# A decode step on one core: TensorE loops over head groups, V gets a single slot, and a group's last sum and mask multiply move behind the next group's first multiply

## The chip, the cores and the metric

The kernel runs on one core of a Trainium2 chip. The time is the device time of one execution in microseconds (us), as the median of several runs. A profile of one execution comes with each kernel; its span (first to last instruction) is 1.1 to 1.3 us shorter than the time.

## The reference

One token of a transformer block is decoded: a layer norm, attention of 32 heads over a cache of 4096 keys and values, and a gated feed-forward part.

```python
x = A_x                                   # (1, 1, 640), bfloat16 as everything
q = layernorm(x) @ wq                     # 32 heads of 128
scores = einsum("bhqd,bhkd->bhqk", q, k_cache) * 128 ** -0.5   # 4096 keys a head
o = einsum("bhqk,bhkd->bhqd", softmax(scores), v_cache)
h = x + o @ wo
out = h + (gelu(n @ w_gate) * (n @ w_up)) @ w_down             # n = layernorm(h), width 1728
```

K and V are 33.6 MB each. With the weights the kernel must read 84.23 MB, and there is only one query row, so every byte is used once.

## The kernel before

The heads are worked in 8 groups of four. A K or V load brings 4 MB, 32 KB to each of 128 partitions; K3 is the K load of group 3. Three slots rotate over all loads; a load into a slot waits until the load three places earlier has been used.

```python
order = [("K", 0), ("V", 0), ("K", 1)]
for G in range(1, NG - 1):
    order += [("K", G + 1), ("V", G)]
order.append(("V", NG - 1))
...   # load n waits for consumed[n - 3]
```

A group has four multiplies on VectorE (`prod`, 128x4096 elements). For each, eight TensorE multiplies with the identity add up the head dimension in part (a "fold"), VectorE sums the rest, and ScalarE takes exponentials in four pieces, each written to its place in a block matrix `p_bd`. The product of these exponentials with V is called P.V; a "head sum" on TensorE then adds up its parts for each head.

Cut to what matters here:

```python
def score_mult(s):
    m = V(tensor_tensor(prod[s % 4], K tile, q))                 # waits: K landed, fold s-4
    folds[s] = T(8 x matmul(ps_f[s % 2], id_b, prod[s % 4]))     # identity loaded 8 times
def score_exp(s):
    reds[s] = V(reduce_sum(sc[s % 4], ps_f[s % 2]))
    for j in range(4):
        A(activation(p_bd[32j:32j+32, G % 2, ..., j], sc[...], Exp, accum_out=RS[...]))
def scores(G):
    for i in range(4):
        score_mult(4 * G + i)
        if i >= 1:
            score_exp(4 * G + i - 1)
    score_exp(4 * G + 3)
...   # program order: scores(G+1), then the P.V product of group G (32 matmuls), then the next group;
...   # group 0's P.V comes before scores(1)
```

After group 3 and after group 7 one half of the heads is normalised and spread for the projection with `wo`. Then follow the second layer norm and the gated part, whose weights are the last loads of the same stream.

The softmax here doesn't subtract the row's maximum and nothing guards it: scores larger than these inputs give would overflow.

## Time and profile before

| | before |
|---|---|
| time, median (lowest to highest) | 203.1 us (202.97 to 203.22) |
| span of the profiled run | 201.9 us |
| HBM bytes read | 84.23 MB, 417 GB/s over the span |
| a group's transfer (K and V) | 19.4 us |
| VectorE busy of that, steady group | 11.5 us |

These lines are from the page of the kernel before: busy time of each engine; the busy tenths and the rate of the DMA engines in 40 equal slices; and the instruction fetches.

```profile
PE 120.4 (60%) x1010; PEld 58.8 (29%) x1010; DVE 101.2 (50%) x106; ACT 61.1 (30%) x273; POOL 5.0 (2%) x14
...
DMA  9999999999999999999999999999999999999992
GB/s 357 414 404 467 428 415 416 422 448 458 430 415 422 415 445 448 435 424 416 422 435 441 438 435 424 416 428 441 448 419 435 399 425 437 419 408 435 412 409 113
...
q8 instruction: 8, 0.13, 0.3%
```

The DMA row is full (9 means 90% or more) from the first slice to the last but one. The windows view gives the busy time of each engine in a stretch. One steady group:

```profile
core 0: us, PE busy (x) PEld busy (x) DVE busy (x) ACT busy (x) POOL busy (x), PEclk, DMA share, GB/s
74.00:93.50 19.50, 11.82 (x72) 5.19 (x72) 11.47 (x8) 7.54 (x34) 0.00 (x0) 0.91 1.01 431
```

The DMA share is 1.01 at 431 GB/s, while no compute engine is busy for more than 12 of 19.5 us. The Trainium skill, "DMA: Bandwidth & Descriptors", section "Where 436 GB/s comes from", puts the ceiling of the ports into SBUF at 435.2 GB/s; this trace runs at 99% of that. The chain of waits that ended last says the same by engine:

```profile
DMA 64%; PE 16%; DVE 14%; issue 3%; SPq 2%
```

The costliest groups of instructions follow (line, engine, operation, shapes, count; busy us and mean ns of one; idle time of the engine just before them and what ended it). VectorE's multiplies waited 31.1 us for K.

```profile
L273 DVE TENSOR_TENSOR prod<-slot,qb 128x4096 bf16<-128x4096 bf16 x32 | 72.4, 2285 | 31.1 <-DMA slot<-in_A_k_cache_dram 31.1
L292 ACT ACTIVATE p_bd<-sc,zero_t 32x32 bf16<-32x32 f32 x128 | 46.4, 362 | 86.3 <-DVE sc L288 85.1
L281 PEld LDWEIGHTS bank<-prod,id_b 128*128 128x128 bf16 x256 | 26.9, 113 | 99.4 <-DVE prod L273 63.1
L288 DVE TENSOR_REDUCE sc<-bank 128x32 f32<-128x512 f32 x32 | 22.0, 688 | 21.4 <-PE bank L281 21.4
```

Last, the timeline of the load queue (SP), the loads V1, K3 and V2, and of VectorE, the first multiply of group 3. The first column is the start in us.

```profile
43.22 0.33 SPq L51 DMA_DIRECT2D slot<-in_A_v_cache_dram  x1
56.43 0.33 SPq L51 DMA_DIRECT2D slot<-in_A_k_cache_dram  x1
69.12 0.33 SPq L51 DMA_DIRECT2D slot<-in_A_v_cache_dram  x1
```

```profile
74.25 4.49 DVE L273 TENSOR_TENSOR prod<-slot,qb 128x4096 bf16<-128x4096 bf16 x2 [2.47 <-DMA slot<-in_A_k_cache_dram]
```

V1 is issued at 43.2 us, long before K2 has landed (about 54 us). V2 is issued 5.1 us before the first multiply on K3 starts.

### The profile page before, as it was taken

Reading aid. Unit: us, or ns where it says so; the run is one execution under the profiler, and the core shown is the slowest. Engines: PE = TensorE matmul, PEld = TensorE weight load, DVE = VectorE, ACT = ScalarE, POOL = GpSimd, SP = SyncE. Lnnn points to the kernel's source line nnn. Section 1 sums busy time; section 2 is a strip of 40 time slices with the busy share of each in tenths; the row PEclk is TensorE's granted clock in tenths of the full one; section 3 lists DMA queues with packets and bytes.
Section 4 is the critical chain, followed back from the end, with each engine's and each line's share of the span. In section 5 each row is a group of like instructions: output and inputs, shape, how many; then the busy total and the mean of one; then the engine's idle time right before and its main releaser. Section 6 shows DMA issues by size and latency. Waiting matters only on the chain.

```text
span 201.9 us, 2505 instructions
## 1 busy us (share of the span) xinstructions
PE 120.4 (60%) x1010; PEld 58.8 (29%) x1010; DVE 101.2 (50%) x106; ACT 61.1 (30%) x273; POOL 5.0 (2%) x14
## 2 busy tenths in 40 slices
PE   0107058537937668690968197727844887467395
PEld 0103023112312233150324032312331344267383
DVE  3201088517979847924791578277708760100221
ACT  2101004620563550670156125603640363100101
POOL 7200000000000000000000000000000000000000
PEclk9999657995799996997599859988995799955555
DMA  9999999999999999999999999999999999999992
GB/s 357 414 404 467 428 415 416 422 448 458 430 415 422 415 445 448 435 424 416 422 435 441 438 435 424 416 428 441 448 419 435 399 425 437 419 408 435 412 409 113
DMA packets 4335, 84.39 MB, mean 418 GB/s; under 512 B 482, under 2 KB 868, under 8 KB 1508
## 3 DMA queue, kind: packets, MB, share of 16 engines
q1 hardware_dynamic: 4322, 84.23, 97.8%
q8 instruction: 8, 0.13, 0.3%
q14 instruction: 3, 0.02, 0.0%
q10 hardware_dynamic: 2, 0.00, 0.0%
HBM read 84.23 MB, written 0.00 MB: 417 GB/s over the span
## 4 chain that ended last, share of the span: by engine, by line
DMA 64%; PE 16%; DVE 14%; issue 3%; SPq 2%
DMA slot<-in_A_k_cache_dram 42%; DVE prod L273 12%; DMA slot<-in_B_w_down_dram 11%; DMA slot<-in_A_v_cache_dram 11%; PE bank L281 11%; PE bank L310 3%; SPq L51 2%; DVE sc L288 2%; PE bank L319 1%; PE bank L447 0%; DVE out_row L460 0%; PE bank L330 0%; DVE RT L329 0%
## 5 line engine op out<-in xcount | busy, mean ns | idle before, releaser
L281 PE MATMUL bank<-prod,id_b 128*128 128x512 bf16 x256 | 75.4, 454 | 50.8 <-DVE prod L273 50.8
L273 DVE TENSOR_TENSOR prod<-slot,qb 128x4096 bf16<-128x4096 bf16 x32 | 72.4, 2285 | 31.1 <-DMA slot<-in_A_k_cache_dram 31.1
L292 ACT ACTIVATE p_bd<-sc,zero_t 32x32 bf16<-32x32 f32 x128 | 46.4, 362 | 86.3 <-DVE sc L288 85.1
L281 PEld LDWEIGHTS bank<-prod,id_b 128*128 128x128 bf16 x256 | 26.9, 113 | 99.4 <-DVE prod L273 63.1
L288 DVE TENSOR_REDUCE sc<-bank 128x32 f32<-128x512 f32 x32 | 22.0, 688 | 21.4 <-PE bank L281 21.4
L292 ACT ACTIVATION_READ_ACCUMULATOR p_bd<-sc,zero_t 32x1 f32 x128 | 23.5, 184 | 0.0
L310 PE MATMUL bank<-slot,p_bd 128*16 128x512 bf16 x256 | 17.3, 379 | 3.1 <-ACT p_bd L292 2.5
L310 PEld LDWEIGHTS bank<-slot,p_bd 128*16 128x16 bf16 x256 | 9.4, 89 | 7.3 <-ACT p_bd L292 3.0
L319 PE MATMUL bank<-po_sb,hs 128*16 128x128 f32 x64 | 8.4, 274 | 1.1 <-ACT po_sb L314 1.1
L348 PE MATMUL bank<-aP,arena 128*128 128x1 bf16 x160 | 6.7, 178 | 3.8 <-DMA arena<-in_A_wo_dram 3.8
L417 PE MATMUL bank<-hlnT,slot 128*128 128x1 bf16 (+1 forms) x140 | 6.7, 176 | 3.2 <-DMA slot<-in_B_w_gate_dram 3.2
L259 PE MATMUL bank<-arena,xlnB 128*32 128x512 bf16 x40 | 3.9, 565 | 7.2 <-DMA arena<-in_A_wq_dram 7.2
L348 PEld LDWEIGHTS bank<-aP,arena 128*128 128x128 bf16 x160 | 6.6, 131 | 3.9 <-DMA arena<-in_A_wo_dram 2.5
L314 ACT COPY po_sb<-bank 128x512 f32<-128x512 f32 x8 | 4.7, 585 | 9.6 <-PE bank L310 9.6
L417 PEld LDWEIGHTS bank<-hlnT,slot 128*128 128x128 bf16 (+1 forms) x140 | 6.3, 118 | 4.1 <-DVE hX L407 3.3
L319 PEld LDWEIGHTS bank<-po_sb,hs 128*16 128x16 f32 x64 | 5.5, 96 | 4.5 <-issue 2.1
L244 ACT ACTIVATE ln<-ln,eps_t 128x1 f32<-128x1 f32 x2 | 0.6, 294 | 20.3 <-DVE ln L242 20.3
L263 DVE CAST qb<-bank 128x512 bf16<-128x512 f32 x1 | 0.7, 692 | 9.6 <-PE bank L259 9.6
L404 DVE TENSOR_TENSOR hT<-xx,bank 128x5 f32<-128x5 f32 x1 | 0.2, 163 | 10.2 <-PE bank L348 10.2
L233 PE MATMUL bank<-one_bf,x_row 1*128 1x1 bf16 x5 | 0.4, 177 | 6.9 <-DMA x_row<-in_A_x_dram 6.9
L259 PEld LDWEIGHTS bank<-arena,xlnB 128*32 128x32 bf16 x40 | 1.6, 136 | 9.1 <-issue 9.0
L334 DVE TENSOR_SCALAR aT<-bank,rz 16x128 bf16<-16x128 f32 x2 | 0.7, 339 | 6.0 <-PE bank L319 6.0
(65 smaller groups left out, 26.3 us busy)
## 6 DMA issues: line engine op xcount, KB each, us to landing
slot<-in_A_k_cache_dram SPq DMA_DIRECT2D x8, 4096.0 KB, 21.4
slot<-in_A_v_cache_dram SPq DMA_DIRECT2D x7, 4096.0 KB, 17.5
arena<-in_A_wq_dram SPq DMA_DIRECT2D x1, 5120.0 KB, 15.4
slot<-in_A_v_cache_dram SPq DMA_DIRECT2D x2, 2048.0 KB, 20.0
arena<-in_A_wo_dram SPq DMA_DIRECT2D x1, 2560.0 KB, 27.3
slot<-in_B_w_gate_dram SPq DMA_DIRECT2D x1, 2160.0 KB, 16.3
arena<-in_A_wo_dram SPq DMA_DIRECT2D x1, 1920.0 KB, 31.5
slot<-in_B_w_up_dram SPq DMA_DIRECT2D x1, 1296.0 KB, 18.4
```

Source lines behind the costliest of these rows:

```text
L51: ev = self.op(eng, lambda e: e.dma_start(out, in_), *deps, dma=True)
L259: i = e.matmul(ps_q[hf][32 * j:32 * j + 32, :], xlnB[:, c, :], wq_j[:, c, j, 4 * hf:4 * hf + 4, :], start=(c == 0), stop=(c == 4))
L263: qa = V(lambda e: e.tensor_copy(qb[:, 0:4, :].rearrange("p g d -> p (g d)"), ps_q[0][:, :]), qd)
L273: m = V(lambda e: e.tensor_tensor(out=prod[:, s % 4, :, :], in0=kt[:, 32 * u:32 * u + 32, :], in1=qb[:, G, :].unsqueeze(1).to_broadcast([1 ...
L281: i = e.matmul(ps_f[s % 2][:, :], id_b[:, :], prod[:, s % 4, :, 16 * b:16 * b + 16], start=(b == 0), stop=(b == 7))
L288: reds[s] = V(lambda e: e.reduce_sum(sc[:, s % 4, :], ps_f[s % 2][:, :].rearrange("p (g d) -> p g d", d=16), axis=AX.X), folds[s], exps.ge ...
L292: x = A(lambda e, j=j: e.activation(p_bd[32 * j:32 * j + 32, G % 2, 32 * (s % 4):32 * (s % 4) + 32, j], sc[32 * j:32 * j + 32, s % 4, :], ...
L310: i = e.matmul(po[a:a + 16, :], p_bd[:, G % 2, 4 * b:4 * b + 4, :].rearrange("p g j -> p (g j)"), vt[:, 4 * b:4 * b + 4, :], start=(b < 4) ...
L314: evs[G] = A(lambda e: e.copy(po_sb[:, G % 2, :], po[:, :]), pvs[G], hds.get(G - 2))
L319: i = e.matmul(ps_a[0:16, 128 * (G // 4):128 * (G // 4) + 128], hs[:, r, 12 - 4 * g:28 - 4 * g], po_sb[:, G % 2, 128 * r:128 * r + 128], s ...
L348: r = e.matmul(ps_p[:, c:c + 1], wo_sb[:, t, i, c::5], aP[:, t, i:i + 1], start=(t == 0 and c == 0 and i == 0), stop=(t == 1 and i == 15), ...
L417: i = e.matmul(ps[0:128 if m < 13 else 64, m:m + 1], ws, hlnT[:, c:c + 1], start=(c == 0 and m == 0), stop=(c == 4), skip_group_check=True)
```

## The change

The change makes the program smaller and takes work out of each group. TensorE's part of groups 1 to 7 becomes a hardware loop that waits on values computed in registers. For that every group must look alike: K has two slots of its own, V has one, the loads go K0 K1 V0 K2 V1 and so on, and group G-1's P.V runs inside group G behind the third fold. The identity stays loaded for a fold. ScalarE takes one 128x128 exponential a group, and VectorE then places it in the block matrix with one mask multiply. The last sum, the exponential and the mask multiply come behind the next group's first multiply. The two half normalisations become one at the end. Cut to its core, in part in words:

```diff
-order = [("K", 0), ("V", 0), ("K", 1)]
+order = [("K", 0), ("K", 1), ("V", 0)]
+k_slot = two slots; v_slot = one slot      # V7 goes to k_slot[0]
+after = mults[4g-5] for K, pvs[g-1] for V  # what a load waits for
...
-for b in range(8): e.matmul(ps_f[s % 2], id_b, prod[...])
+first matmul loads id_b, seven more keep it (held)
...
-for j in range(4): A(activation(p_bd[32j:32j+32, ...], sc[...], Exp, accum_out=RS[...]))   # per quarter group
+exps[G]   = A(activation(pt[:, G % 2, :], sc[:, G % 2, :], Exp, accum_out=RS[:, G]))       # per group
+blocks[G] = V(tensor_tensor(p_bd, pt (broadcast x4), own (mask), mult))                    # 128x512
...
 def scores(G):
     for i in range(4):
         mults[4G+i] = V(tensor_tensor(prod[i], K, q))
         if i >= 1: reduce(G, i - 1)
+        elif G >= 1: probs(G - 1)      # last sum, exponential, mask multiply of the group before
...
+lp = P.loop("tensor", range(1, NG), [head sum of k-2, fold 0, fold 1, fold 2, P.V of k-1, fold 3])
```

## The prediction

> **What bounds the kernel now.** The input stream. The row of DMA busy tenths shows 9 in every slice but the last, and the windows view gives a DMA share of 1.00 and 428 to 435 GB/s in each stretch of about 19.5 us from 55 us to 171.4 us. The bytes are fixed: 84.23 MB read. The Trainium skill, "DMA: Bandwidth & Descriptors", section "Where 436 GB/s comes from", puts the fabric ceiling at 435.2 GB/s; this trace agrees (429 in mid-stream). An estimate from these: 84.23 MB / 432 GB/s = 195 us, plus about 1 us before the first packet, about 1 us lost in the slow first slices (357 GB/s), about 2.7 us from the last landing (199.2) to the end, plus 1.1 us between span (201.9) and time (203.0). Almost nothing is left to win. One head group needs 19.5 us of K and V transfer; VectorE works 11.5 to 12 us of that, TensorE about 12, ScalarE 7. VectorE's idle time is waiting for K (31.1 us).
>
> **What the change removes, adds, moves.**
> - ScalarE: 128 exponentials of 362 ns with 128 accumulator reads become 8: about 5.8 us a group becomes about 0.6. Off the critical path.
> - TensorE: the identity of a fold is loaded once, not 8 times (113 ns each, overlapped). The loop cuts its instructions about in half. Off the path.
> - VectorE: a mask multiply of 128x512 a group, estimated at 0.3 to 0.7 us from the 128x512 cast (0.69 us); 12 becomes about 12.6 us of 19.5.
> - The last sum, the exponential and the mask multiply now stand behind the next group's first multiply, so they and the P·V product wait for the next K.
> - Instruction fetches: 8 packets (0.13 MB) become about 4, worth 0.2 us (estimate: 4 x 0.6 us of one of 16 engines, if the slowest engine gains). Back-branches could refetch (the skill, "Runtime: NRT & Kernel Launch", section "Instruction fetch mechanics", warns of branches that leave the fetched window); no run shows this yet.
>
> **Does the stream run dry?** Two K slots and one V slot: a V load waits for the previous group's P·V, which runs after the third fold of the group whose K has just landed. With multiply 2.28, sum 0.69, fold 1.9 and P·V 1.9 us, the V load is issued 13 to 14 us after K lands; the queue empties 19.5 us after it. That leaves 4 to 5 us of reserve, similar to before, where V loads go out 12 to 15 us after K lands. Tightest is the beginning: groups 0 and 1 run back to back, P·V of group 0 ends near 51, V1 must be queued by about 53. A cold TensorE or a costly loop entry could open a gap of 0 to 2 us there.
>
> **The end.** V7, wo, gate, up and down keep order and bytes. The last down landing (199.2) and the TensorE chain before it (ends 199.1) stay co-critical. One combined finish after V7 replaces the half done early, but wo lands at 177.5, near aP (175.2), with 2 us spare.
>
> **Predicted:** 202.7 us, range 201.9 to 204.0. Faster by over 2%: 0.01; within 2%: 0.95; slower: 0.04.
>
> **What would show it.** DMA 9 in all slices, 429 GB/s in mid-stream; VectorE's wait for K still about 25 to 31 us; no DMA gap near 54 us; ScalarE busy near 20 us instead of 61; fewer instruction packets.
>
> **What would make it wrong.** Loop or register waits costing over 4 us a group, or refetched instructions, so that V loads are issued late and the stream has holes; a stall on entering the loop.

## The result

The changed kernel takes 203.11 us (median of 4 runs, 202.93 to 203.78) against 203.1 us. The ratio is 1.0006, with a 95% interval of 0.9989 to 1.0023: the same.

The page after:

```profile
PE 121.9 (60%) x1002; PEld 36.9 (18%) x778; DVE 105.7 (52%) x114; ACT 12.6 (6%) x33; POOL 2.4 (1%) x8
...
DMA  9999999999999999999999999999999999999992
GB/s 357 415 398 468 429 422 416 422 442 465 377 455 422 422 422 444 429 455 422 422 422 435 442 429 442 429 422 416 448 429 448 393 432 427 427 408 440 409 411 105
...
q8 instruction: 4, 0.07, 0.1%
```

ScalarE's busy time fell from 61.1 to 12.6 us and the weight loads' (PEld) from 58.8 to 36.9, mostly since a fold loads the identity once and not eight times (32 loads of L346 for 256 of L281, below and above); the instruction packets went from 8 to 4. The DMA row and the span did not move. The windows view, first the stretch that turns out to matter and then the steady group:

```profile
50.00:60.00 10.00, 6.00 (x36) 1.24 (x10) 4.68 (x5) 1.08 (x3) 0.00 (x0) 0.88 1.01 421
74.00:93.50 19.50, 12.22 (x72) 2.15 (x44) 11.99 (x9) 1.08 (x3) 0.00 (x0) 0.78 1.00 432
```

The DMA share is 1.00 again in the steady group, and the rate the same. PEclk, the clock granted to TensorE, is lower there (0.78 against 0.91), as it is over the whole span in all four runs (0.79 to 0.81; the kernel before had 0.82 to 0.87 in the runs of e1's rounds). No run here tests whether the change causes that. The chain of waits, and the groups that answer to those shown of before:

```profile
DMA 60%; DVE 20%; PE 11%; SPq 6%; ACT 1%; issue 1%
```

```profile
L377 DVE TENSOR_TENSOR prod<-k_slot,qb 128x4096 bf16<-128x4096 bf16 x32 | 73.0, 2285 | 43.4 <-DMA k_slot<-in_A_k_cache_dram 43.4
...
L369 DVE TENSOR_REDUCE sc<-bank 128x32 f32<-128x512 f32 x32 | 21.9, 686 | 3.8 <-PE bank L167 3.8
L346 PEld LDWEIGHTS bank<-prod,id_b 128*128 128x128 bf16 x32 | 3.1, 98 | 102.5 <-DVE prod L377 99.5
...
L394 DVE TENSOR_TENSOR p_bd<-pt,own 128x512 bf16<-128x512 bf16 x8 | 5.5, 693 | 4.5 <-ACT pt L392 4.5
...
L392 ACT ACTIVATE pt<-sc,zero_t 128x128 bf16<-128x128 f32 x8 | 3.2, 402 | 71.7 <-DVE sc L369 71.7
```

The mask multiply (L394) takes 693 ns. VectorE's wait for K grew from 31.1 to 43.4 us, and its sums' wait for folds shrank from 21.4 to 3.8: the late last sum turned one wait into the other. Together 52.5 us of idle before, 47.2 after; VectorE's busy time grew by 4.5 us and a wait of 4.5 us for the exponential is new. Nothing of this shows in the time. Now the load queue, V1, K3 and V2, and the first multiplies on K2 and K3:

```profile
50.53 0.33 SPq L59 DMA_DIRECT2D v_slot<-in_A_v_cache_dram  x1
50.91 0.89 SPq L59 DMA_DIRECT2D k_slot<-in_A_k_cache_dram  x1
67.75 0.33 SPq L59 DMA_DIRECT2D v_slot<-in_A_v_cache_dram  x1
```

```profile
54.76 2.29 DVE L377 TENSOR_TENSOR prod<-k_slot,qb 128x4096 bf16<-128x4096 bf16 x1 [4.75 <-DMA k_slot<-in_A_k_cache_dram]
...
74.20 2.29 DVE L377 TENSOR_TENSOR prod<-k_slot,qb 128x4096 bf16<-128x4096 bf16 x1 [6.89 <-DMA k_slot<-in_A_k_cache_dram]
```

K3 is used at 74.20 us, as before (74.25). But V1 is issued at 50.5 us and not at 43.2. The packet records of the trace (not shown; they are in the trace file) hold sixteen 4-byte packets at the end of each load. Taken as one for each of the 16 DMA engines, they say that the first engine has finished K2 at 52.4 us. In a run below where the queue was found empty, the first packet came 0.95 us after the start of the issue. So V1 was due near 51.5 us, and it came 0.9 us early; call that its reserve. The next, V2, is issued 6.45 us before K3 is used; the first engine is through with K3 at 72.1 us, so its reserve is about 3.4 us. Reckoned in the same way, V2 of the kernel before (issued at 69.1, first engine through at 71.9) had 1.8 us, and its V1 8.3 us; V3 to V6 had 4.4 to 4.6 us before and have 3.3 to 3.4 now. That the changed kernel's V1 was close fits its first packets: of 16, six took 1.55 to 2.05 us, where 1.21 us is usual (V2's took 1.22 at most).

### The profile page after: what moved, and what is told of

It reads as the page before. It is cut to its first block, busy times and chain, and to the rows that moved or that the text cites. A ratio compares the mean times of both kernels' runs of the same rounds, so it can differ in the third digit from the quotient of the medians. Undisturbed runs are those within 1.5% of the kernel's fastest.

```text
span 201.7 us, 2059 instructions
## 1 busy us (share of the span) xinstructions
PE 121.9 (60%) x1002; PEld 36.9 (18%) x778; DVE 105.7 (52%) x114; ACT 12.6 (6%) x33; POOL 2.4 (1%) x8
## 4 chain that ended last, share of the span: by engine, by line
DMA 60%; DVE 20%; PE 11%; SPq 6%; ACT 1%; issue 1%
DMA k_slot<-in_A_k_cache_dram 49%; DVE prod L377 15%; DMA k_slot<-in_B_w_down_dram 11%; SPq L59 6%; PE bank L167 6%; PE bank L353 4%; DVE sc L369 3%; DVE p_bd L394 1%; PE bank L346 1%; ACT pt L392 1%; PE bank L521 0%; DVE out_row L534 0%
## 5 line engine op out<-in xcount | busy, mean ns | idle before, releaser
L377 DVE TENSOR_TENSOR prod<-k_slot,qb 128x4096 bf16<-128x4096 bf16 x32 | 73.0, 2285 | 43.4 <-DMA k_slot<-in_A_k_cache_dram 43.4
L167 PE MATMUL bank<-prod,id_b 128*128 128x512 bf16 x224 | 66.7, 448 | 0.0
L346 PE MATMUL bank<-prod,id_b 128*128 128x512 bf16 x32 | 14.9, 465 | 53.3 <-DVE prod L377 53.0
L346 PEld LDWEIGHTS bank<-prod,id_b 128*128 128x128 bf16 x32 | 3.1, 98 | 102.5 <-DVE prod L377 99.5
L353 PE MATMUL bank<-v_slot,p_bd 128*16 128x512 bf16 x224 | 13.3, 379 | 0.0
L359 PEld LDWEIGHTS bank<-hs,po_sb 128*128 128x128 f32 x72 | 10.2, 207 | 13.3 <-issue 10.0
L359 PE MATMUL bank<-hs,po_sb 128*128 128x4 f32 x72 | 9.5, 255 | 0.7 <-ACT po_sb L366 0.7
L491 PE MATMUL bank<-hlnT,v_slot 128*128 128x1 bf16 (+1 forms) x140 | 6.7, 176 | 3.0 <-DMA v_slot<-in_B_w_gate_dram 3.0
L353 PEld LDWEIGHTS bank<-v_slot,p_bd 128*16 128x16 bf16 x224 | 5.0, 89 | 17.6 <-issue 12.8
L394 DVE TENSOR_TENSOR p_bd<-pt,own 128x512 bf16<-128x512 bf16 x8 | 5.5, 693 | 4.5 <-ACT pt L392 4.5
L491 PEld LDWEIGHTS bank<-hlnT,v_slot 128*128 128x128 bf16 (+1 forms) x140 | 6.3, 118 | 3.9 <-DVE hX L481 3.1
```

What stands on the lines that cost most here:

```text
L167: built = e.matmul(out, lhsT, rhs, start=start, stop=stop)
L346: mm = held if b else lambda e, *a, **k: e.matmul(*a, **k)
L353: i = e.matmul(ps_o[a:a + 16, :], p_bd[:, 4 * b:4 * b + 4, :].rearrange("p g j -> p (g j)"), vt[:, 4 * b:4 * b + 4, :], start=(b < 4), sto ...
L359: i = e.matmul(ps_a[:, bass.ds(at, 4)], po_sb[:, 128 * r:128 * r + 128], hs[:, r, :], start=(r == 0), stop=(r == 3))
L377: mults[s] = VS(lambda e, i=i: e.tensor_tensor(out=prod[:, i, :, :], in0=kt[:, 32 * i:32 * i + 32, :], in1=qb[:, G, :].unsqueeze(1).to_bro ...
L394: blocks[G] = VS(lambda e: e.tensor_tensor(out=p_bd[:, :, :], in0=pt[:, G % 2, :].unsqueeze(2).to_broadcast([128, 128, 4]), in1=own[:, :]. ...
```

## The experiments

The theory: the input stream sets the time; the work taken off the engines was never on the path, and what the change adds stays hidden as long as each load is issued before the DMA engines run dry. The first rival: the change did shorten the groups, and one of its own parts (the late mask multiply, the loop, the single V slot) gave the gain back. The second rival: the stream only looks full.

Each kernel ran 4 times against the kernel before on the same chip (three chips in all; the kernel before took 203.2 us on each). All passed the comparison with the reference, even those whose result is wrong; the comparison with this input is too coarse to notice them.

### e1: a quarter of the multiplies' width

```diff
-out=prod[:, i, :, :],   in0=kt[:, 32*i:32*i+32, :], in1=q (32 wide)
+out=prod[:, i, 0:8, :], in0=kt[:, 32*i:32*i+8, :],  in1=q (8 wide)    # the rest of prod is zeroed once
```

> The changed kernel with each score multiply cut to a quarter of its width (wrong result on purpose; the rest of the product buffer is zeroed once). VectorE work falls by about 32 x 1.7 = 54 us, the bytes stay. Theory (the input stream sets the time, everything else hides under it): time 203.1 +- 0.5 us, VectorE's wait for K grows from 43 us to about 95 us. Rival (the change shortened the groups and something it added, the waits of the late mask multiply or of the single V slot, gave that back, so group work still counts): time falls by 4 us or more.

Measured: 202.98 us, ratio to before 0.9986 (0.9966 to 1.0006). VectorE's busy time fell by 49.4 us, to 56.3. The groups of VectorE's sums and multiplies:

```profile
L370 DVE TENSOR_REDUCE sc<-bank 128x32 f32<-128x512 f32 x32 | 22.1, 689 | 24.8 <-PE bank L167 24.8
L378 DVE TENSOR_TENSOR prod<-k_slot,qb 128x1024 bf16<-128x1024 bf16 x32 | 21.8, 684 | 71.5 <-DMA k_slot<-in_A_k_cache_dram 71.5
```

49 us of work bought nothing. The first rival falls as far as VectorE's group work goes: there was no hidden gain to pay back. The size of the wait for K was expected too high (95 us), because the sums now wait 24.8 us for folds.

### e2: sum, exponential and mask multiply at the end of their own group

```diff
         if i >= 1: reduce(G, i - 1)
-        elif G >= 1: probs(G - 1)
+    probs(G)
```

> The changed kernel with the last sum, the exponential and the mask multiply put back at the end of their own group. V loads go out 1.5 to 2 us earlier (11 to 11.5 us after K lands, not 13). Theory (stream): 203.1 +- 0.4 us, no gain, since the reserve was not used up. Rival (the late position costs time): 1 us or more faster.

Measured: 205.07 us, ratio 1.0089 (1.0068 to 1.011). This is a miss, and the most useful one. In the steady groups V is issued 12.5 to 12.7 us after the first multiply on K, against 13.0 in the changed kernel; 11 to 11.5 was expected, but VectorE's sums wait for folds again (27.8 us). There is still reserve there. But groups 0 and 1 run back to back, and there the old position makes VectorE wait for the fold and then for the exponential between the groups. Group 1 starts at 40.4 us and not at 36.9, and V1 is issued here:

```profile
52.91 0.33 SPq L59 DMA_DIRECT2D v_slot<-in_A_v_cache_dram  x1
```

```profile
50.00:60.00 10.00, 6.81 (x57) 1.87 (x42) 7.18 (x6) 0.96 (x3) 0.00 (x0) 0.97 0.93 365
```

That is 1.4 us after it was due. The share of the DMA engines between 50 and 60 us falls to 0.93 (1.01 in the changed kernel). The packet records of the trace show V1's first packets at 53.9 us, and the first 16 of them took 1.7 to 2.2 us, not 1.21. On average an engine stood idle for 1.2 us after K2, and its first packet of V1 took 0.8 us longer than usual. Every later load ends 1.6 us later than in the changed kernel on average over the engines, and the last packet of the stream 2.0 us later: the stream loses time once and never makes it up.

### e9: e2 with the P.V product one fold earlier

```diff
-fold 0, fold 1, fold 2, P.V of k-1, fold 3
+fold 0, fold 1, P.V of k-1, fold 2, fold 3
```

> As e2 (sum and mask multiply at the end of their own group, which cost 2 us), and P.V moved one fold earlier in TensorE's loop, so V1 is issued near 50 us again and not at 52.9. If e2 lost its 2 us only because V1 missed the moment at which the queue runs dry (first engines done with K2 at 52.4 us, about 1 us from issue to first packet, so V1 must be issued by about 51.4): 202.9 to 203.5 us and no hole near 53 us. Rival (the position at the end of the group costs time in every group): 205 us as in e2.

```profile
49.86 0.33 SPq L59 DMA_DIRECT2D v_slot<-in_A_v_cache_dram  x1
```

```profile
50.00:60.00 10.00, 6.90 (x29) 1.65 (x10) 8.04 (x6) 0.96 (x3) 0.00 (x0) 0.81 0.99 416
```

Measured: 203.35 us, ratio 1.0015 (0.9998 to 1.0031). V1 is back at 49.9 us, the DMA share is 0.99, and all but about 0.3 us of e2's loss is gone. So the position at the end of the group costs nothing by itself that these runs can resolve; it counts through the moment at which V1 is issued. With P.V behind the third fold, as in the change, the late position is what lets V1 go out in time; e9 shows that an earlier P.V does so as well.

### e10: the changed kernel with the loads K0 V0 K1

```diff
-order = [("K", 0), ("K", 1), ("V", 0)]
+order = [("K", 0), ("V", 0), ("K", 1)]
```

> The changed kernel with the first three loads in the order of before: K0 V0 K1. Bytes and work are the same. The P.V of group 0 stands behind the third fold of group 1, and K1 now lands near 44.5 us and not 35, so V1 goes out near 57.5 us, some 6 us after the 51.4 at which it is due. Theory (the load order is what pays for the late P.V and the single V slot): one hole near 53 us as in e5b, whose V1 went out at 57.5: 207.5 to 209.5 us. Rival (the order is of no matter, the stream is full): 203.1 us.

```profile
57.82 0.33 SPq L59 DMA_DIRECT2D v_slot<-in_A_v_cache_dram  x1
```

```profile
50.00:60.00 10.00, 8.42 (x64) 1.74 (x41) 9.94 (x8) 0.59 (x1) 0.00 (x0) 0.99 0.44 162
```

Measured: 209.54 us, ratio 1.0313 (1.0296 to 1.033), at the upper end of what was expected. Same bytes, same work, but V1 leaves over 6 us after it was due, and the DMA engines are busy 0.44 of the time between 50 and 60 us. The first K3 multiply comes at 79.7 us, 5.5 us late. The new load order is therefore no detail: it pays for the single V slot and the late P.V.

### e4, e5: idle multiplies before each P.V in the loop

```diff
 fold 0, fold 1, fold 2,
+16 (e4) or 32 (e5) x matmul(bank[4], id_b, ones_b[:, 0:512])
 P.V of k-1, fold 3
```

> The changed kernel with 16 idle multiplies (about 3.4 us) put before each P.V in TensorE's loop, so each V load is issued 3.4 us later. The trace gives a reserve of about 5.4 us in the steady groups (19.4 us between two K landings, V issue 13.0 us after the first, about 1 us from issue to first packet) and about 3.2 us for V1. Theory (stream with that reserve): 203.1 to 203.8 us, V issue 16.4 us after K. Rival (the reserve is already gone and V loads come just in time): 7 x 3.4 = 24 us slower.

> The changed kernel with 32 idle multiplies (about 6.8 us) before each P.V. By the reserves first read from the trace, 3.2 us (V1) and 5.4 us (V2 to V6), the stream would have holes of 3.6 us once and 1.4 us five times: 212 to 216 us. Half of that delay has already cost 5.4 us where 0 to 0.7 was expected, so the reserve is smaller than it was read, or the idle multiplies take longer; if it is about 2 us less, holes of about 5.5 us once and 3.5 us five times: 222 to 228 us. Rival (TensorE's idle time takes it): 203 us.

Measured: e4 208.57 us, ratio 1.0268 (1.0237 to 1.0299); e5 218.17 us, ratio 1.0742 (1.0698 to 1.0787). Both are misses on size. In e4 the 16 idle multiplies take 3.6 us (25.3 us in seven passes). V1 goes out at 53.6 us, and V3 to V6 16.4 us after the first multiply on a K (13.0 undelayed), here K3 and V3:

```profile
75.53 2.29 DVE L377 TENSOR_TENSOR prod<-k_slot,qb 128x4096 bf16<-128x4096 bf16 x1 [7.78 <-DMA k_slot<-in_A_k_cache_dram]
```

```profile
91.97 0.33 SPq L59 DMA_DIRECT2D v_slot<-in_A_v_cache_dram  x1
```

The distances between the first multiplies on K2, K3 and so on to K7 are 20.6, 20.1, 19.4, 20.5 and 19.6 us where 19.4 is the stream's own pace. The reserve was read too large, 5.4 us for V2 to V6 and 3.2 us for V1. The mistake was to take a K's landing as the moment at which the queue runs dry: the first engines are through some 2 us before VectorE starts on that K. Corrected by that, the reserves are 3.4 and 0.9 us, and a delay of 3.5 us just overruns the larger one. In e5 the loss at V1 is 5.0 us and the mean of the four later steps 20.9 us. That is less than expected even with the smaller reserve, because a hole also puts off the moment at which the next load is due: by the packet records V2 and V4 came about in time, and V3, V5 and V6 2.5, 1.7 and 0.7 us late. The rival, that the V loads come just in time everywhere, would have cost e4 about 24 us.

### e6: the kernel before with 32 idle multiplies before each P.V

> The kernel before with the same 32 idle multiplies before each P.V. There a K load waits for that P.V, and it has about 10 us of reserve; V loads wait for multiplies and have 6.7 us (3.1 us for V2), moved by under 1 us. Theory (the single V slot has shortened the reserve without showing in the time): 203.1 to 204 us here, against over 212 for the changed kernel. Rival (both kernels have the same reserve): both slow down alike.

Measured: 213.94 us, ratio 1.0522 (1.0486 to 1.0558). This is a miss of the experiment's design. In the kernel before, the idle multiplies also stand in front of the P.V of groups 6 and 7 at the end, one after the other, and the loads of `w_down` and `w_gate` wait behind that. TensorE's timeline, and the windows view of the same stretch:

```profile
180.87 6.85 PE L306 MATMUL bank<-ones_b,id_b 128*128 128x512 bf16 x31 [0.16 <-issue]
187.65 1.90 PE L312 MATMUL bank<-slot,p_bd 128*16 128x512 bf16 x32
```

```profile
185.00:195.00 10.00, 8.80 (x134) 5.63 (x133) 0.58 (x4) 0.58 (x1) 0.00 (x0) 0.97 0.44 143
```

The DMA share is 0.44 there. The two kernels were not delayed in the same places, so their times cannot be compared. What remains is the pace in the middle: from the first multiply on K3 to that on K7 a group takes 20.0 us here and 20.9 us in e5 (19.4 undelayed in both). So even in the middle the delay cost the kernel before something (0.6 us a group against 1.5). That fits a larger reserve, but this run does not show it: TensorE has up to 7 us more to do in each of these groups.

### e3: the loop written out

```diff
-with e.Fori(1, NG) as k: body(k)
+for k in range(1, NG): body(k)          # waits on constants
```

> The changed kernel with TensorE's loop written out seven times. Instruction packets go from 4 to 7 or 8, instructions up by some 900. Theory (stream): 203.1 to 203.3 us, at most 0.2 us slower from the fetches. Rival (the loop's branches and register waits cost time that the rest of the change earned): 0.5 us or more faster.

Measured: 203.58 us, ratio 1.0015 (0.9987 to 1.0043), with 7 instruction packets and not 4. The median is 0.3 us above the expected range, but the interval does not tell it from the changed kernel. So the loop costs nothing that can be seen, and earns nothing that can be seen. In the profiled run the first multiply on K3 comes 0.8 us later than in the changed kernel, and by the packet records one of the 16 DMA engines is later with it than the others by 0.7 us; why, these runs do not settle.

### e7, e8, e11, e12: short loads, so that the work is no longer hidden

To see what the change does to the work itself, every K and V load from the fourth on, except the last V, was cut to a quarter of its bytes (wrong results), in both kernels and with both load orders.

```diff
-w = 128 * DH // parts
+w = 128 * DH // parts // (1 if first three or last load else 4)
```

> The kernel before with every K and V load from the fourth on, except the last V, cut to a quarter of its bytes (wrong result on purpose: the rest of the slot holds old data), so that group work is no longer hidden. Estimate: K1 lands at 44.5, then 12.8 us a group, then the rest of the stream: 162 to 169 us.

> The changed kernel with the same loads cut. K1 lands at 34.8 us, so group 1 starts at 37 and not at 44.6; a group takes about 12.6 us (the late last sum saves a wait of 1.4 us for the fold, the mask multiply and its wait cost 1.25 us). Estimate 155 to 161 us, some 7 us faster than the kernel before so cut, nearly all of it from the load order. Rival (the 48 us taken off ScalarE are worth something once the stream is out of the way): more than 12 us faster.

> The kernel before with short loads as in e7b (172.5 us) and the first three loads in the order of the change: K0 K1 V0, nothing else of the change. Theory (of the 11.4 us between e7b and e8b, about 7.7 come from the order alone, since group 1 starts at 37 and not at 44.6; the group period is 12.7 against 12.6): 163 to 166 us. Rival (the gain comes from the work taken off the engines): 171 to 173 us.

> The changed kernel with short loads as in e8b (161.1 us) and the first loads in the order of before: K0 V0 K1. Theory (order alone): group 1 starts 7.6 us later, 168 to 170 us, so the rest of the change keeps 3 to 4 us over e7b. Rival (the work taken off the engines is the gain): 161 to 163 us.

| time, us | K0 V0 K1 | K0 K1 V0 | the order gives |
|---|---|---|---|
| kernel before | 172.48 (e7) | 165.79 (e11) | 6.7 |
| changed kernel | 167.84 (e12) | 161.08 (e8) | 6.8 |
| the rest of the change gives | 4.6 | 4.7 | |

All four differ from 203 us by far: with fewer bytes and the same multiplies they are 31 to 42 us faster, so the second rival falls. e7 is a miss (162 to 169 us expected), and e12 lies just under its range. The 11.4 us between e7 and e8 lie between e8's theory (some 7) and its rival (more than 12), so e11 and e12 were run to part them. The two parts add up. The order lets group 1 start at 37 to 39 us and not at 44.5. For the rest, here is VectorE's timeline in e7, from one group's first multiplies over the last sum (idle time before it in brackets) to the next group's:

```profile
72.81 4.48 DVE L273 TENSOR_TENSOR prod<-slot,qb 128x4096 bf16<-128x4096 bf16 x2
...
84.88 0.69 DVE L288 TENSOR_REDUCE sc<-bank 128x32 f32<-128x512 f32 x1 [1.40 <-PE bank L281]
85.49 4.48 DVE L273 TENSOR_TENSOR prod<-slot,qb 128x4096 bf16<-128x4096 bf16 x2
```

and in e8, over the mask multiply. The first and last rows are the first multiplies of two groups:

```profile
62.62 2.28 DVE L379 TENSOR_TENSOR prod<-k_slot,qb 128x4096 bf16<-128x4096 bf16 x1
...
66.21 0.69 DVE L396 TENSOR_TENSOR p_bd<-pt,own 128x512 bf16<-128x512 bf16 x1 [0.56 <-ACT pt L394]
...
75.22 2.28 DVE L379 TENSOR_TENSOR prod<-k_slot,qb 128x4096 bf16<-128x4096 bf16 x1
```

A group takes 12.68 us before and 12.60 us after. Even with the stream out of the way, the 48 us taken off ScalarE buy next to nothing: VectorE is the next limit, and there the late last sum saves a wait of 1.40 us for the fold while the mask multiply and the wait for the exponential take almost all of it back. The 4.6 us come from elsewhere. From group 1 to group 7, e7 takes 80.9 us and e12 75.5. Of that difference of 5.4, the first two groups account for 3.2 (14.0 and 14.2 us, each with a second wait of 1.3 to 1.4 us for a fold), and the two groups with the half normalisation of the heads for 2.1 (13.3 and 14.0 us); after group 7, e12 takes 0.7 us longer.

## Why the prediction was right

The time was predicted at 202.7 us (201.9 to 204.0), as the same; it is 203.11. Point by point:

- *"What bounds the kernel now. The input stream."* Right. The DMA share is 1.00 in the middle before and after, and e1 shows that 49 us of VectorE work can go without moving the time.
- *"128 exponentials ... become 8 ... Off the critical path."* Right, and more so than said: e7 and e8 show it off the next limit too. ScalarE's busy time was predicted near 20 us and is 12.6.
- *"a mask multiply of 128x512 a group, estimated at 0.3 to 0.7 us"*: 0.693 us, as the cast of that size. VectorE's steady group went from 11.5 to 12.0 us (predicted: from 12 to about 12.6).
- *"VectorE's wait for K still about 25 to 31 us"*: wrong, 43.4. The prediction forgot that the late last sum takes away the wait for folds (21.4 to 3.8 us), and that this idle time then shows as wait for K.
- *"That leaves 4 to 5 us of reserve, similar to before"*: mis-sized. It is 3.3 to 3.4 us for V2 to V6 (e4's delay of 3.5 us just overran it), because the engines run dry about 2 us before VectorE starts on the K, and the first packet needs 0.95 us.
- *"V1 must be queued by about 53"*: the place was right, the term too large. It was due near 51.5 us; it went at 50.5. e2, with V1 at 52.9, lost 2 us. That kept to the predicted bound of 53 and still left the predicted range (205.07 us). So the number was right in part by luck: it stood on a reserve of 0.9 us, where the prediction counted on about 2 (P.V ends near 51, bound near 53).
- *"Back-branches could refetch"*: they did not; the looped kernel fetched 4 packets, the unrolled one 7. A fetch packet took 1.0 to 1.1 us, not the 0.6 estimated; the predicted gain of 0.2 us from fewer fetches is below what these runs resolve.
- *"wo lands at 177.5, near aP (175.2), with 2 us spare"*: `aP` is done at 177.1 us, and TensorE starts the projection at 177.6. The spare time was 0.5 us, since the last half of P.V and its head sum took 1.9 us each (1.04 and 1.05 before), while TensorE was granted a clock of 0.58 between 169 and 176 us (0.98 before).

So the work taken off gave nothing, as predicted: it was never on the path. No version that reads all its bytes beats both kernels. e1, with far less work, is at 0.9986 of before with an interval that includes 1; by the prediction's estimate, some 195 of the 203 us are the stream itself.

## What to carry to other kernels

When the input stream is full, count a change by when it lets each load be issued, not by the work it removes: 48 us off ScalarE gave nothing, and a V load 2.4 us later cost 2 us. Measure a reserve from the moment the first DMA engine is through with the queued load, not from the landing that a compute engine sees. Parts of a change can be each other's price: here the single V slot and the late P.V keep the time only with the new load order (e10), and equal times hide that the smallest margin of a load fell from 1.8 us (V2) to 0.9 us (V1).

## What the Trainium skill lacked or had wrong

- "DMA: Bandwidth & Descriptors", specifications table and "Where 436 GB/s comes from": HBM to SBUF is said there, without a condition, to be bound near 358 GB/s per core. Here one core reads 428 to 435 GB/s in the middle of the stream, which agrees with the same page's 425 GB/s measured on a single core and with its ceiling of 435.2. A note between the two on that page keeps the 358 for the case that both cores of a pair stream; the section should say so too.
- The same page gives a first-byte latency of about 0.6 us. This agrees if it is counted from the end of the issue (0.33 us): 0.95 us from its start in e2. The page lacks what restarting a drained queue costs beyond that: in e2 the first 16 packets of 32 KB took 1.7 to 2.2 us where 1.21 us is usual.
- The same page gives no figure for how far apart the 16 engines finish one load: in the changed kernel they finished K2 between 52.4 and 54.3 us, and VectorE began on it at 54.76.
- "Runtime: NRT & Kernel Launch", section "Instruction fetch mechanics", warns that a taken branch breaks the prefetch when its target is outside the fetched window, and has no case of one inside. Here a TensorE loop of seven passes fetched 4 packets in all, against 7 unrolled, and no time for it can be seen (203.11 and 203.58 us, not told apart).
